# Values three tokens in a row, keys at every third column, and a work order with chance in it

## Chip, cores and metric

The kernel runs on one core of one Trainium2 chip. The metric is the device time of one execution in microseconds (us); the profile shows one such execution, with a span of 1484.0 us and a granted TensorE clock of 0.997 of full speed.

## The reference

Two blocks follow one another. The first is attention over 8 batches, 12 heads, 448 tokens and 64 features, in which queries and keys are first normalised by their root mean square:

```python
q_n, k_n = rmsnorm(q, g_q), rmsnorm(k, g_k)      # x / sqrt(mean(x*x) + 1e-6) * g
scores = q_n @ k_n.T / sqrt(64)
attn = softmax(scores)                            # over the keys
x = (attn @ v), heads side by side                # (3584, 768)
g = x @ w_gate                                    # 768 -> 1536
out = (silu(g) * (x @ w_val)) @ w_out             # 1536 -> 768
```

All inputs are float32 except the three weight matrices, which come as float64 (two 32-bit words each).

The softmax sums over all keys of a head, so the order in which keys are laid out does not matter as long as the values are laid out in the same one. The change rests on this.

## The kernel before

`fast` does the work; `general` is a second version behind a test on the gains, and does not run with these inputs.

**Attention.** Work goes by pairs of heads: 8 x 6 = 48 pairs, `attention(m)`. For a pair, q and k are loaded in pieces of 32 tokens by 32 features (`load`, L728), squared on ScalarE (L754), summed on VectorE (L768) and between partitions on ScalarE (L778, then L782), turned into inverse roots (L678 to L686), scaled on GpSimd (L795), transposed on VectorE in blocks of 32 (L811), and the queries are multiplied by the gains on ScalarE (L814). Now features lie on partitions, 64 for each of the two heads, and tokens along the row: `KT` and `QT`.

The 448 tokens are cut into chunks of 128, 128, 128 and 64 (j = 0 to 3). `scores(j)` (L840) makes the scores of one chunk of keys against all queries, transposed: keys on partitions, queries along the row. Keys are the stationary operand, 64 columns of `KT` at a time, x = 0, 1 for the halves of a chunk and h = 0, 1 for the heads, so four 64x64 matmuls fill the four quadrants of TensorE's array at once. A float32 product takes two passes, so each appears as two weight loads and two matmuls in the trace. ScalarE takes the exponentials (L855), and `weighted(j)` (L916) multiplies them by the values, again in quadrants. The values of a pair are in the tile `v`, tokens on partitions in the same chunks (`load_values`, L744 and L747): token 128 j + p is on partition p. The sums of the exponentials come from a product with a constant (`total`, L947), are inverted (L982), spread over the features (L990 in the first twelve pairs, L1000 after them) and multiplied in (L1005 copies, L1008 joins, L1012 divides).

**Feed-forward.** It goes by blocks of two batches, NB = 4. Its products use a fast matrix multiplication with 15 products for a 3x3 block split; sums of blocks of x are made in `sides` (L1049, L1053), sums of weight blocks once at the start in `convert`, which also turns float64 words into float32 on ScalarE (L1146, L1150) and VectorE (L1168 to L1180), adds on GpSimd (L1202) and stores to DRAM (L1227). There are 24 conversions. The up products are at L1328, the down products at L1502; VectorE and ScalarE read their banks (L1270 to L1276), and results are transposed (L1550) and stored (L1560).

**Stages.** The first 12 pairs run beside the first conversions; then the up products of block 0 beside the other conversions; then the down products of block n beside the 12 pairs for block n + 1, in turn with the up products of block n + 1; last the down products of block 3.

**The order of the work.** Nothing is emitted where it is written. Each piece is given to `Order.add` with its engine, an estimate of its length (`us`), the pieces it comes after, the buffers it takes out of a ring (`takes`) or uses, a due time (`when`) and a `rank`. `Order.run` then plays the program through by these estimates. Pieces of an engine are sorted by `key`, due time less rank. Of an engine's pieces that can start, the first by that key is chosen, unless a later one can start more than 0.4 us earlier; among engines, the earliest start goes first, and within 0.3 us the smaller key. Pieces are emitted in the order in which they are chosen, and that is the order of each engine's queue. Attention pieces of the first twelve pairs mostly have rank 60, reads of the up banks 60, reads of the down banks 20, conversions 20 or, for the first six (`by_bank` false), 0.

## Time and profile before

| what | value |
|---|---|
| time, three runs | 1485.67, 1486.94, 1488.83 us; median 1486.94 |
| span of the profiled execution | 1484.0 us |
| TensorE (PE) busy | 1425.0 us, 96% |
| VectorE (DVE) busy | 916.0 us, 62% |
| ScalarE (ACT) busy | 681.5 us, 46% |
| GpSimd (POOL) busy | 414.1 us, 28% |
| start of the first matmul | 14.7 us |
| start of the first up product | 140.1 us |
| DMA packets | 415921, of these 324164 under 512 bytes |

PE is TensorE's matmul side and PEld its weight loads, which overlap matmuls. SPq is SyncE, which issues most DMAs in a queue of its own. Busy time in a group of instructions is the time in which at least one of them ran; "idle before" is the engine's idle time just ahead of them, with what ended it after the arrow. In a list of waits the columns are the total in us, how many, and the longest one. In a table by stage the numbers after the engines are the granted clock, the mean share of 16 DMA engines, and GB/s.

### The profile page before, as it was taken

Reading aid. Unit: us, or ns where it says so; the run is one execution under the profiler, and the core shown is the slowest. Engines: PE = TensorE matmul, PEld = TensorE weight load, DVE = VectorE, ACT = ScalarE, POOL = GpSimd, SP = SyncE. Lnnn points to the kernel's source line nnn. Section 1 sums busy time; section 2 is a strip of 40 time slices with the busy share of each in tenths; the row PEclk is TensorE's granted clock in tenths of the full one; section 3 lists DMA queues with packets and bytes.
Section 4 is the critical chain, followed back from the end, with each engine's and each line's share of the span. In section 5 each row is a group of like instructions: output and inputs, shape, how many; then the busy total and the mean of one; then the engine's idle time right before and its main releaser. Section 6 shows DMA issues by size and latency. Waiting matters only on the chain.

```text
span 1484.0 us, 19470 instructions
## 1 busy us (share of the span) xinstructions
PE 1425.0 (96%) x6672; PEld 675.4 (46%) x6672; DVE 916.0 (62%) x1405; ACT 681.5 (46%) x1366; POOL 414.1 (28%) x468
## 2 busy tenths in 40 slices
PE   5789999999999999999999999999999999999998
PEld 2334544443444455544444445554444445555553
DVE  4777887877978544355886733454786854432533
ACT  6774544437775322445767422354676532122100
POOL 2454586636444100012544200011343410000000
PEclk9999999999999999999999999999999999999999
DMA  7767999974453432533344432352353442222235
GB/s 165 158 144 236 292 308 341 296 219 90 99 115 85 113 106 71 138 103 90 74 111 110 100 117 73 106 136 77 96 119 85 90 119 89 80 98 73 83 98 107
DMA packets 415921, 193.30 MB, mean 130 GB/s; under 512 B 324164, under 2 KB 397892, under 8 KB 409668
## 3 DMA queue, kind: packets, MB, share of 16 engines
q1 hardware_dynamic: 402688, 190.35, 48.0%
q10 hardware_dynamic: 12996, 1.61, 0.7%
q8 instruction: 55, 0.90, 0.3%
q14 instruction: 54, 0.44, 0.1%
q0 software_dynamic: 128, 0.00, 0.0%
HBM read 157.29 MB, written 34.60 MB: 129 GB/s over the span
## 4 chain that ended last, share of the span: by engine, by line
PE 73%; DVE 3%; ACT 2%; issue 1%; DMA 1%; SPq 1%; ACTq 0%; DVEq 0%
PE mm L1502 22%; PE mm L1328 20%; PE at L1328 20%; PE st L840 6%; PE at L916 5%; PE st L947 1%; ACT spare L1000 1%; ACT es L855 1%; DVE rd L982 1%; DMA out_dram<-spare 0%; SPq L728 0%; DVE ss L782 0%; DMA work<-in_k_dram 0%; DVE ss L768 0%; DVE sums L866 0%
## 5 line engine op out<-in xcount | busy, mean ns | idle before, releaser
L1328 PE MATMUL mm<-xs,ws 128*128 128x448 f32 x960 | 401.2, 540 | 4.4 <-DVE spare L1276 2.2
L1328 PE MATMUL at<-xs,ws 128*128 128x448 f32 x960 | 400.6, 540 | 4.1 <-DVE v L1274 2.6
L1328 PEld LDWEIGHTS mm<-xs,ws 128*128 128x128 f32 x960 | 181.5, 190 | 185.8 <-issue 173.8
L1328 PEld LDWEIGHTS at<-xs,ws 128*128 128x128 f32 x960 | 181.9, 190 | 184.6 <-issue 172.6
L795 POOL TENSOR_TENSOR work<-work,rr 128x448 f32<-128x448 f32 x96 | 105.9, 1122 | 503.5 <-DVE rr L686 245.2
L840 PE MATMUL st<-work 64*64 64x448 f32 (+1 forms) x1536 | 155.1, 508 | 27.3 <-ACT work L814 21.2
L1502 PE MATMUL mm<-gt,ws 128*128 128x448 f32 x448 | 177.2, 545 | 0.0
L1272 DVE TENSOR_TENSOR gt<-gt,mm 128x448 f32<-128x448 f32 x64 | 39.7, 621 | 185.1 <-PE mm L1328 171.3
L1502 PE MATMUL mm<-hs,ws 128*128 128x448 f32 x384 | 152.1, 545 | 0.9 <-DVE ss L684 0.9
L855 ACT ACTIVATE es<-st 128x896 f32<-128x896 f32 x129 | 114.3, 913 | 56.1 <-PE at L916 42.8
L860 POOL TENSOR_TENSOR sums<-es 128x896 f32<-128x896 f32 x36 | 75.7, 2104 | 195.8 <-PE st L947 83.2
L1402 ACT ACTIVATE st<-gt 128x448 f32<-128x448 f32 x96 | 52.4, 547 | 163.8 <-DVE gt L1276 85.9
L1000 ACT COPY spare<-rd 32x224 f32<-32x224 f32 x288 | 108.1, 375 | 35.0 <-DVE rd L982 30.7
L1502 PEld LDWEIGHTS mm<-gt,ws 128*128 128x128 f32 x448 | 82.9, 190 | 84.2 <-issue 81.0
L916 PE MATMUL at<-es,v 64*64 64x448 f32 x1032 | 110.2, 545 | 7.2 <-ACT xs L1005 3.3
L1270 ACT COPY gt<-mm 128x448 f32<-128x448 f32 x80 | 42.5, 531 | 141.5 <-PE mm L1328 141.4
L1502 PEld LDWEIGHTS mm<-hs,ws 128*128 128x128 f32 x384 | 71.1, 190 | 72.9 <-issue 70.9
L840 PEld LDWEIGHTS st<-work 64*64 64x64 f32 x1536 | 50.9, 134 | 108.7 <-issue 38.1
L1270 ACT COPY v<-at 128x448 f32<-128x448 f32 x96 | 51.1, 532 | 83.2 <-PE at L1328 80.0
L860 POOL TENSOR_TENSOR sums<-sums,es 128x896 f32<-128x896 f32 x36 | 78.7, 2187 | 2.8
L811 DVE STREAM_TRANSPOSE work<-work 128x448 f32<-128x448 f32 x96 | 59.2, 627 | 25.2 <-POOL work L795 23.1
L916 PEld LDWEIGHTS at<-es,v 64*64 64x64 f32 x1032 | 39.7, 134 | 67.4 <-issue 57.4
(150 smaller groups left out, 1568.7 us busy)
## 6 DMA issues: line engine op xcount, KB each, us to landing
ws<-up_sides SPq DMA_DIRECT2D x32, 1024.0 KB, 4.9
ws<-down_sides SPq DMA_DIRECT2D x16, 1024.0 KB, 5.0
ws<-down_sides SPq DMA_DIRECT2D x28, 512.0 KB, 4.0
ws<-up_sides SPq DMA_DIRECT2D x16, 768.0 KB, 4.6
work<-in_q_dram SPq DMA_DIRECT2D x192, 56.0 KB, 2.4
work<-in_k_dram SPq DMA_DIRECT2D x188, 56.0 KB, 2.5
out_dram<-spare SPq DMA_DIRECT2D x168, 56.0 KB, 1.9
v<-in_v_dram SPq DMA_DIRECT2D x96, 96.0 KB, 2.5
```

What stands on the lines that cost most here:

```text
L795: nc.gpsimd.tensor_tensor(out=tiles["t", m][:, x], in0=tiles["qk", (m, x)], in1=rr.to_broadcast([P, NC, C]), op=ALU.mult,)
L811: nc.vector.transpose(to, tiles["t", m][:, x].rearrange("p c f -> p (c f)"))
L840: nc.tensor.matmul(st[ds(D * x, D), h, 0:n], tiles["KT", m][rows, ds(P * j + D * of_keys, D)], tiles["QT", m][rows, ds(Q * of_queries, n)] ...
L855: nc.scalar.activation(e, tiles["st", (m, j)][:, :, 0 : S * width(j) // P], AF.Exp)
L860: nc.gpsimd.tensor_tensor(out=to, in0=tiles["e", (m, 0)] if j == 1 else to, in1=e, op=ALU.add)
L916: nc.tensor.matmul(tiles["at", (m, x)][ds(D * h, D), queries], tiles["v", m][rows, j, h], tiles["e", (m, j)][rows, h], start=j == 0, stop= ...
L1000: nc.scalar.copy(inv[ds(D * h + C * to, C), ts(x, Q)], tiles["rd", m][ds(D * h + C * x, C)])
L1270: nc.scalar.copy(to, ps)
L1272: nc.vector.tensor_tensor(out=to, in0=old, in1=ps, op=ALU.add)
L1328: nc.tensor.matmul(ps(), w[:, at, which, c], xs[:, SLOT[x], c], start=fresh and c == 0, stop=c == NC2 - 1, skip_group_check=True,)
L1402: nc.scalar.activation(take(*act, [P, 2, TB])[:, 0, 0:S], to, AF.Silu)
L1502: nc.tensor.matmul(banks[s][:, 0:S], w[:, at, s, g], where[x][:, g], start=fresh and g == 0, stop=g == NG - 1, skip_group_check=True,)
```

## The change

There are three edits.

First, the layout of the values. For the first three chunks, token 3 p + j now goes to partition p of chunk j, so that three tokens that follow one another in memory, 768 bytes, land in one partition's row. The tile is now partition, head, chunk, feature, and one DMA does both heads, where two with rows of 256 bytes were needed. The last 64 tokens stay as they were, loaded twice, once for either half. The estimate of the load goes from 2.4 to 1.8 us.

Second, the keys have to follow: the keys of chunk j, half x, are columns 192 x + j, 192 x + j + 3, and so on, 64 of them, every third column of `KT`. Queries keep their place, so outputs do too.

Third, the order. Every piece that takes no buffer out of a ring gets a shift drawn from -3 to 3 us, added to its key; the draw has a fixed seed, one chosen out of eighty. All conversions have rank 20.

```diff
+        self.chance = random.Random(9)
...
+            shift=self.chance.uniform(-3.0, 3.0) * (not takes),
...
     def key(self, piece):
-        return piece["when"] - piece["rank"], piece["n"]
+        return piece["when"] - piece["rank"] + piece["shift"], piece["n"]
...
         def load_values():
-            x = take("v", m, [P, NJ, 2, D])
-            for h in range(2):
-                rows = v[b, 2 * c + h][0 : P * (NJ - 1)]
-                nc.sync.dma_start(x[:, 0 : NJ - 1, h], rows.rearrange("(j p) d -> p j d", p=P))
+
+            x = take("v", m, [P, 2, NJ, D])
+            rows = v[b][2 * c : 2 * c + 2, 0 : P * (NJ - 1)]
+            nc.sync.dma_start(
+                x[:, :, 0 : NJ - 1].rearrange("p h j d -> p h (j d)"),
+                rows.rearrange("h (p j) d -> p h (j d)", p=P),
+            )
             rows = v[b][2 * c : 2 * c + 2, P * (NJ - 1) :].rearrange("h s d -> s h d")
             for p in (0, D):
-                nc.sync.dma_start(x[ds(p, D), NJ - 1], rows)
-
-        load_v = add("SP", 2.4, ready - 16.0, load_values, takes=[("v", m)], kb=256, early=25.0)
+                nc.sync.dma_start(x[ds(p, D), :, NJ - 1], rows)
+
+        load_v = add("SP", 1.8, ready - 16.0, load_values, takes=[("v", m)], kb=256, early=25.0)
...
                 of_keys, of_queries = (x, 0) if j < NJ - 1 else (0, x)
+                keys = ds(P * j, D)
+                if j < NJ - 1:
+                    keys = slice(
+                        (NJ - 1) * D * x + j, (NJ - 1) * (D * x + D - 1) + j + 1, NJ - 1
+                    )
...
-                        tiles["KT", m][rows, ds(P * j + D * of_keys, D)],
+                        tiles["KT", m][rows, keys],
...
-                        tiles["v", m][rows, j, h],
+                        tiles["v", m][rows, h, j],
...
-        rank = 20.0 if by_bank else 0.0
+        rank = 20.0
```

More of the change, by code (lines that the diff above doesn't have):

```diff
@@ L358, in general @@
             fn()
+import random
 class Order:
```

## The prediction

> **What bounds the kernel now.** I read the engine totals first, then the stages, then who ends the tensor engine's waits, then the loads of the values.

> ```profile
> PE 1425.0 (96%) x6672; PEld 675.4 (46%) x6672; DVE 916.0 (62%) x1405; ACT 681.5 (46%) x1366; POOL 414.1 (28%) x468
> PE 73%; DVE 3%; ACT 2%; issue 1%; DMA 1%; SPq 1%; ACTq 0%; DVEq 0%
> ```

> TensorE is busy for 1425.0 of 1484.0 us, and the chain of waits runs through it. No edit removes or adds a matmul, so the change can only move the 59.0 us in which TensorE is idle, or add idle. Where these lie is told by the busy time by stage (columns: stage, length, then busy us of PE, PEld, DVE, ACT, POOL):

> ```profile
> 15.00:141.00 126.00, 106.21 (x1198) 46.83 (x1190) 95.20 (x158) 86.24 (x163) 62.38 (x94) 0.99 0.72 175
> 141.00:350.00 209.00, 200.50 (x575) 98.78 (x578) 167.25 (x251) 95.43 (x145) 121.82 (x222) 1.00 0.90 274
> 350.00:505.00 155.00, 151.85 (x1016) 64.00 (x1008) 124.86 (x182) 105.50 (x242) 71.29 (x42) 1.00 0.46 102
> ```

> TensorE stands idle 126 - 106.2 = 19.8 us while the first twelve pairs run beside the first weights, 8.5 us in the first block's up products beside the rest of the weights, and 3.2 us in the first mixed stage. Ahead of the first matmul lie 14.7 us and after the last one 7.4 us of stores; both are latency that no edit touches. What is left for all of 505 to 1476 us is 59.0 - 14.7 - 19.8 - 8.5 - 3.2 - 7.4 = 5.4 us. So an order can win at most 19.8 + 8.5 + 3.2 = 31.5 us, nearly all before 350 us. The first matmul's own wait is the 14.7 in the list of waits:

> ```profile
> PE st L840 <- ACT work L814: 21.2, 6, 14.7
> PE at L916 <- ACT xs L1005: 3.3, 2, 2.3
> PE at L916 <- DVE xs L1008: 2.7, 2, 2.1
> PE at L916 <- ACT gt L855: 2.3, 2, 1.3
> PE mm L990 <- DVE rd L982: 2.0, 2, 1.3
> ```

> The other 6.5 us of the first line, and the next four, are waits for the queries' copy, the copy and the join of the sums, an exponential and a reciprocal: short pieces on ScalarE and VectorE that stood behind other work on a strict queue. VectorE is busy for 95.2 and ScalarE for 86.2 of 126 us there, so neither is full; it is their order that lets TensorE wait.

> [...] 190 ns for 128 columns, 134 for 64, 107 for 32 (next fence and its group at L947), so (190 - 134) / 64 = 0.88 ns a column on top of some 78 ns. [...] by its packet records one of 256 bytes takes 18 ns, of 512 bytes 27, of 1024 bytes 46 (medians).

> **The change part by part.**

> *Keys every third column.* Three chunks x two halves x two heads x two passes = 24 of the 32 score loads of a pair, 1152 of these 1536:

> ```profile
> L840 PEld LDWEIGHTS st<-work 64*64 64x64 f32 x1536 | 50.9, 134 | 108.7 <-issue 38.1 <-ACT work L814 26.7 <-ACT es L855 16.6
> L1328 PEld LDWEIGHTS mm<-xs,ws 128*128 128x128 f32 x960 | 181.5, 190 | 185.8 <-issue 173.8
> ```

> The lower end is nothing. For the upper end I double the 56 ns that depend on the columns: 190 ns, just what a 128-column load takes now. Four quadrants load together, once for four matmuls that occupy 376 ns (timeline: sets start every 0.375 us, their loads end after 0.15 us and the load row then idles 0.22 us "issue"). So a load even of 190 ns hides inside a set. It shows only where the slot is short: at the entry from full products, and after the half-wide fourth chunk, whose sets last 0.19 us: two places a pair, 2 x 48 x 56 ns = 5.4 us. I take a quarter, 1.3 us; range 0 to 5.4.

> *Values three tokens in a row.*

> ```profile
> L744 SPq DMA_DIRECT2D v<-in_v_dram x96: 378/484/3534, 7.5 to 1173.4; - x96
> L747 SPq DMA_DIRECT2D v<-in_v_dram x96: 595/607/1903, 8.6 to 1174.6; - x96
> ```

> A pair costs SyncE 2 x 0.484 + 2 x 0.607 = 2.2 us; one issue goes, so 1.7. Its 1024 packets of 256 bytes (1.15 us over 16 engines) become 256 of 768 and 256 of 256; with 36 ns for 768 bytes, between 27 and 46, that is 0.58 + 0.29 = 0.87. So 0.48 us of queue and 0.28 us of transfer go per pair. Where would it show? In the first stage SyncE's queue is the busiest thing but TensorE (in 60:100 its issues leave some 7 us free), and each q and k load queues behind one for values. Twelve pairs x 0.48 = 5.8 us of queue. Yet TensorE waits for no load there, and the squares at L754, the first use of q and k, wait for landings only 8.1 us in all, off TensorE's path by two to three pairs of depth. I take -1 us; bounds 0 and -5.8. In the 36 later pairs q, k and v come long before use: nothing.

> *Half the memory layout.* The weighted sum's loads read rows of 64 adjacent values either way: nothing changes.

> *Converting rank 20 for all.* Only the first six conversions had rank 0. Attention pieces of the first stage have rank 60, so they still go first in a tie; the six move ahead only of things ranked below, of which there are hardly any before 75 us. I take 0, bounds -2 to +2.

> *The order by chance.* Up to 3 us earlier or later in the key of every piece that takes no buffer: squares of the second tensor, roots, scales, the queries' transposes, joins, divides, sides, conversions, and products. A shift decides only between pieces that could start within 0.3 to 0.4 us of each other (that is how run() chooses), so chains stay as they are and full products, tied one to the next, keep their order. Reads of the banks with rank 60 stay ahead. What can change is what stands in front of L814, L1005, L1008 and L982 on ScalarE and VectorE: exactly the owners of the waits above. Such a piece is delayed by one other, by what the rows cost: a conversion's 1.28 us on ScalarE, 1.05 us or 0.75 us on VectorE, an exponential's 0.91. With five to seven waits of 1.0 to 2.3 us (the longest in the list) removed, or as many added, this is worth some 7 to 10 us either way. An arbitrary order would have no sign; one kept out of eighty leans to the good side, if what it was kept by resembles the chip. I take -7: a quarter of 31.5 (7.9), less a little that returns as a wait elsewhere.

> Sum: +1.3 - 1 + 0 - 7 = -6.7, so 1486.9 - 6.7 = **1480 us**.

> **Rivals.** *Order gains nothing net*: the stage is held by VectorE with its 95 us plus latencies, a wait removed returns at the next piece; the parts cancel to about -0 to +1: 1487. For it: several engines are within 30% of each other in the first stage. Against: each single wait has another owner. *Large gain*: half of the 31.5 us goes and SyncE's relief shows, -15.7 - 1: 1470. For it: the engines have room of 30 to 40 us in 15:141. Against: the latency of a pair's chain, square to exponential, repeats whatever the order. *Slower*: an order made for estimates that the chip doesn't keep; first-stage waits grow by a third (+6.6), the loads cost their upper 5.4, the values' gain is hidden: +12, less a little, 1496. It is made likelier by shifts that also act on later stages, which now lose only 5.4 us and so can only get worse.

> **How the numbers follow.** Forecast (3 to 12 us gained) 0.46; large gain 0.16; nothing (within 3 us) 0.14; slower 0.24. So faster 0.62, same 0.14, slower 0.24. The range leaves out about one in ten on either side: 1469 to 1495, the first short of the full large gain, the second close to the upper costs together.

> **What would show it.** Right: TensorE's idle time in 15:350 falls from 28 us to about 21, first product (L1328) starts before 140 us, the waits for L814, L1005 and L1008 shrink; L840's loads stay below 190 ns and the time of score groups unchanged; later stages as before, 190 us from one mixed stage's start to its end. Wrong: L840's loads of 250 ns or more, and gaps ahead of matmuls inside a score group in all three mixed stages, would make the strided keys the main thing; new waits after 505 us would blame the order; a first product later than 141 us with more waits at L1005 or L814 would be the slower rival.

## The result, and the profile after

The change makes the kernel slower: 1501.51 us in the median of four runs (1497.27 to 1503.44), against 1486.69 for the kernel before on the same chip. The ratio is 1.0094, with a 95% interval from 1.0067 to 1.012. The forecast of 1480 and its whole range lie below that.

The profiled execution took 1497.27 us. These are the engine totals, and the table by stage, of the kernel after:

```profile
span 1495.5 us, 19454 instructions
PE 1434.1 (96%) x6672; PEld 690.3 (46%) x6672; DVE 917.7 (61%) x1405; ACT 687.0 (46%) x1370; POOL 409.5 (27%) x468
```

```profile
15.00:141.00 126.00, 108.50 (x1196) 50.81 (x1197) 91.88 (x156) 86.19 (x165) 62.63 (x94) 0.97 0.68 169
141.00:350.00 209.00, 196.02 (x526) 96.39 (x526) 162.12 (x248) 93.72 (x136) 116.33 (x220) 0.97 0.89 273
350.00:505.00 155.00, 149.04 (x994) 65.99 (x993) 120.96 (x167) 105.37 (x240) 73.42 (x44) 0.99 0.43 93
```

The reader is to see two things. TensorE's busy time rose by 1434.1 - 1425.0 = 9.1 us although the number of matmuls, 6672, is the same; its idle time rose only by 11.5 - 9.1 = 2.4 us. And the granted clock, the number after POOL, fell from 0.99, 1.00, 1.00 to 0.97, 0.97, 0.99. The matmuls themselves became slower.

The record of the granted clock in the trace says how. Ahead of the stores at the end, the kernel before has one stretch at half clock, of 3.41 us, at 97.6 us. The kernel after has seven of them, at 31.7, 65.9, 141.0, 270.7, 321.9, 342.3 and 403.8 us. Six more stretches of 3.41 us at half speed can cost up to 6 x 3.41 / 2 = 10.2 us. Each begins within 1.1 us of the end of a wait of TensorE of 1.9 to 3.2 us. The list of TensorE's waits after, from 141 to 350 us, has the longest of these:

```profile
PE st L853 <- ACT work L822: 3.2, 1, 3.2
PE at L1341 <- DVE v L1285: 2.8, 1, 2.8
PE mm L1341 <- DVE gt L1285: 2.8, 1, 2.8
PE at L1341 <- DVE v L1289: 2.6, 1, 2.6
```

(L840 is L853 after the change, L916 L929, L1328 L1341, L1502 L1515, L1272 L1285.) What stood in front is seen in the timeline of the second line, each row with start and length. The product that begins at 260.95 us has ended at 262.62, but VectorE reads its bank only at 269.28; the rows between are conversions, which stood ahead in VectorE's queue (four of them are shown). The next product of that bank has to wait for the read, until 269.95:

```profile
260.95 1.67 PE L1341 MATMUL at<-xs,ws 128*128 128x448 f32 x4
...
266.22 0.76 DVE L1193 CUSTOM_DVE_ANT_0 hs<-hs,st 128x1152 uint16<-128x1152 uint16 x1 [0.17 <-POOL spare L1215]
...
267.01 0.76 DVE L1181 TENSOR_SCALAR st<-hs 128x576 uint32<-128x576 uint32 x1
...
267.81 0.76 DVE L1187 SCALAR_TENSOR_TENSOR st<-hs,st 128x576 uint32<-128x576 uint32 x1
...
268.61 0.75 DVE L1193 CUSTOM_DVE_ANT_0 hs<-hs,st 128x1152 uint16<-128x1152 uint16 x1
269.28 0.61 DVE L1285 TENSOR_TENSOR v<-v,at 128x448 f32<-128x448 f32 x1
...
269.95 1.94 PE L1341 MATMUL at<-xs,ws 128*128 128x448 f32 x3 [2.82 <-DVE v L1285]
```

The busy time by short stages around it shows what follows (the granted clock is the number after POOL). From 271 to 274 us TensorE is always busy, but only six matmuls touch these 3 us, where at 376 ns apart eight would begin:

```profile
267.00:269.00 2.00, 0.13 (x1) 0.00 (x0) 1.92 (x3) 0.00 (x0) 1.84 (x5) 1.00 0.81 311
270.00:271.00 1.00, 1.00 (x3) 0.49 (x4) 0.97 (x2) 0.00 (x0) 0.92 (x2) 0.83 1.03 382
271.00:274.00 3.00, 3.00 (x6) 1.34 (x5) 1.73 (x3) 2.46 (x3) 2.84 (x7) 0.50 1.07 355
```

The texts put on record call such a stretch a half-clock window. Longer ones in the runs below are 6.83, 10.24 and 17.07 us, two, three and five times 3.41. The waits here, 1.9 to 3.2 us, are shorter than the stretch that followed them.

Not every long wait is paid for in this way, and the traces tell which is. In each of the 17 traces of this page the recorded changes of the clock are whole multiples of 3.4133 us apart, to within 3 ns (from the first to the last of the kernel after it is 1460.90 us, 428 times that), so that a trace can be cut into steps of this length. In the kernel after, each of the seven stretches follows a step in which TensorE was idle, by the profile's times of its matmuls, for 2.2 to 3.0 us in all. Three other waits, of 2.6, 2.6 and 2.0 us (ending at 132.5, 289.6 and 366.4 us), lie across the edge of a step, leave at most 1.9 us of idle time in one step, and no half clock follows them. Over all traces together, ahead of the stores at the end, half clock followed a step at full clock with more than 2.02 us of idle time in 61 of 61 cases, one with less than 1.49 us in none of 7027, and one in between in 23 of 63. In the traces of before and after alone it followed each of 8 steps with 2.18 us or more and none of 841 with 1.91 or less.

Where the loss arises is told by the starts of products in the traces (us; the columns are the runs of this page):

| start of | before | after | layout_only | est_only | late_shift_old_start |
|---|---|---|---|---|---|
| first up product | 140.1 | 141.1 | 137.8 | 170.6 | 138.4 |
| first down product | 329.7 | 343.8 | 328.8 | 360.6 | 327.6 |
| up products of block 1 | 505.1 | 520.7 | 504.9 | 530.9 | 504.1 |
| up products of block 2 | 855.3 | 868.8 | 855.6 | 880.8 | 852.2 |
| up products of block 3 | 1205.7 | 1217.2 | 1206.3 | 1230.8 | 1200.6 |
| end | 1484.0 | 1495.5 | 1484.6 | 1509.0 | 1478.9 |

After the change 15.6 us are lost before block 1, 13.1 of them between the first up product and the first down product, and 4.1 us are won in blocks 1 and 2. Single executions differ at the start: the six traces whose compute engines have the order of `layout_only` up to block 1 (that run, `late_shift_old_start` and the four `stall` runs) begin block 1 between 503.2 and 508.9 us. The losses shown here are larger than that.

The weight loads of the scores, and below them the loads of values in `layout_only`, with the shortest, median and longest issue in ns:

```profile
L853 PEld LDWEIGHTS st<-work 64*64 64x64 f32 x1536 | 59.1, 157 | 103.3 <-issue 31.8 <-ACT work L822 30.1 <-ACT es L868 9.6
```

```profile
L749 SPq DMA_DIRECT2D v<-in_v_dram x48: 378/397/4406, 7.5 to 1173.5; - x48
```

The mean of a weight load went from 134 to 157 ns over all 1536 loads. With 133 ns for the 384 of the fourth chunk, the 1152 with every third column take (1536 x 157 - 384 x 133) / 1152 = 165 ns. That is 32 ns more for 64 columns. The kernel before has no load with every third column, so its trace could not show this; why such a load takes longer, no run shows.

### The profile page after: what moved, and what is told of

It reads as the page before. It is cut to its first block, busy times and chain, and to the rows that moved or that the text cites. A ratio compares the mean times of both kernels' runs of the same rounds, so it can differ in the third digit from the quotient of the medians.

```text
span 1495.5 us, 19454 instructions
## 1 busy us (share of the span) xinstructions
PE 1434.1 (96%) x6672; PEld 690.3 (46%) x6672; DVE 917.7 (61%) x1405; ACT 687.0 (46%) x1370; POOL 409.5 (27%) x468
## 4 chain that ended last, share of the span: by engine, by line
PE 74%; DVE 2%; ACT 1%; issue 1%; DMA 1%; DVEq 0%; ACTq 0%
PE mm L1515 23%; PE mm L1341 19%; PE at L1341 19%; PE st L853 7%; PE at L929 6%; PE st L960 1%; DMA out_dram<-spare 0%; ACT es L868 0%; DVE ss L689 0%; ACT spare L1013 0%; DVE rd L995 0%; DVE spare L1563 0%; ACT work L822 0%; DVE rr L691 0%; DVE ss L776 0%
## 5 line engine op out<-in xcount | busy, mean ns | idle before, releaser
L1341 PE MATMUL mm<-xs,ws 128*128 128x448 f32 x960 | 404.8, 544 | 6.4 <-DVE gt L1285 2.8
L1341 PE MATMUL at<-xs,ws 128*128 128x448 f32 x960 | 401.9, 541 | 5.5 <-DVE v L1285 2.8
L1341 PEld LDWEIGHTS mm<-xs,ws 128*128 128x128 f32 x960 | 182.6, 191 | 190.4 <-issue 173.8
L1341 PEld LDWEIGHTS at<-xs,ws 128*128 128x128 f32 x960 | 182.5, 191 | 186.4 <-issue 174.8
L803 POOL TENSOR_TENSOR work<-work,rr 128x448 f32<-128x448 f32 x96 | 99.9, 1059 | 527.2 <-DVE rr L691 300.1
L853 PE MATMUL st<-work 64*64 64x448 f32 (+1 forms) x1536 | 157.1, 515 | 32.0 <-ACT work L822 24.9
L1515 PE MATMUL mm<-gt,ws 128*128 128x448 f32 x448 | 175.2, 543 | 0.0
L1285 DVE TENSOR_TENSOR gt<-gt,mm 128x448 f32<-128x448 f32 x64 | 39.7, 620 | 198.6 <-PE mm L1341 173.4
L1515 PE MATMUL mm<-hs,ws 128*128 128x448 f32 x384 | 153.6, 552 | 0.0
L1515 PEld LDWEIGHTS mm<-gt,ws 128*128 128x128 f32 x448 | 83.7, 190 | 83.7 <-issue 81.3
L929 PE MATMUL at<-es,v 64*64 64x448 f32 x1032 | 112.7, 542 | 4.2 <-DVE xs L1021 4.2
L853 PEld LDWEIGHTS st<-work 64*64 64x64 f32 x1536 | 59.1, 157 | 103.3 <-issue 31.8
L1515 PEld LDWEIGHTS mm<-hs,ws 128*128 128x128 f32 x384 | 72.4, 193 | 73.7 <-issue 72.4
L929 PEld LDWEIGHTS at<-es,v 64*64 64x64 f32 x1032 | 40.9, 134 | 63.5 <-issue 59.5
```

The lines of the kernel that those rows point to most:

```text
L803: nc.gpsimd.tensor_tensor(out=tiles["t", m][:, x], in0=tiles["qk", (m, x)], in1=rr.to_broadcast([P, NC, C]), op=ALU.mult,)
L853: nc.tensor.matmul(st[ds(D * x, D), h, 0:n], tiles["KT", m][rows, keys], tiles["QT", m][rows, ds(Q * of_queries, n)], start=True, stop=True,)
L929: nc.tensor.matmul(tiles["at", (m, x)][ds(D * h, D), queries], tiles["v", m][rows, h, j], tiles["e", (m, j)][rows, h], start=j == 0, stop= ...
L1285: nc.vector.tensor_tensor(out=to, in0=old, in1=ps, op=ALU.add)
L1341: nc.tensor.matmul(ps(), w[:, at, which, c], xs[:, SLOT[x], c], start=fresh and c == 0, stop=c == NC2 - 1, skip_group_check=True,)
L1515: nc.tensor.matmul(banks[s][:, 0:S], w[:, at, s, g], where[x][:, g], start=fresh and g == 0, stop=g == NG - 1, skip_group_check=True,)
```

## Experiments

The first two split the change into its layout and its order. `layout_only` has the new layout of values and keys, and on every compute engine the order of the kernel before, piece for piece; `order_only` has the order of the kernel after with the old layout.

```diff
 layout_only (against the kernel after):
+            shift=0.0,
+        load_v = add("SP", 2.4, ready - 16.0, load_values, ...
+        rank = 20.0 if by_bank else 0.0
```

> The new layout of values and keys, with the order of the kernel before, piece for piece, on every compute engine (no shifts, old ranks, old estimate of the load). Theory A (the new order's waits before 505 us, and the half-clock windows that follow them, are the loss): 1485 to 1490 us, one or two half-clock windows, score weight loads 157 ns in the mean. Rival B (the weight loads with every third column hold the tensor engine up): 1495 us or more, at full clock.

Measured 1485.36 us, ratio to before 0.9984 [0.9974, 0.9995]; two half-clock stretches ahead of the end. The layout costs nothing on balance; it gains some 2 us (0.7 to 3.9 by the interval).

> The new order on every compute engine, with the old layout of values and keys. Theory A: 1496 to 1504 us, six or more half-clock windows, waits of 2.5 to 3.2 us for VectorE while the first block's up products run. Rival B: 1483 to 1490 us.

Measured 1504.80 us, just above theory A's range; ratio 1.0132 [1.0101, 1.0164], seven stretches ahead of the end. The whole loss is the order's. Strided keys, rival B, are out.

The order has three causes: shifts, rank, and the plan's estimate of the load. In `no_chance` only the shifts are taken out of the kernel after; in `chance_late` they act only late:

```diff
 chance_late:
-            shift=self.chance.uniform(-3.0, 3.0) * (not takes),
+            shift=self.chance.uniform(-3.0, 3.0) * (not takes) * (when >= 490.0),
```

> The changed kernel with all shifts at zero: new layout, load estimated at 1.8 us, rank 20 for all conversions. Theory A: 1482 to 1491 us, close to before, since the shifts and not the ranks or the estimate made the waits. Rival C (rank or estimate moved the order as much as the shifts): 1495 us or more, or a first stage unlike that of before.

Measured 1499.60 us, ratio 1.0079 [1.0061, 1.0098]. My theory A fell in this part: without a single shift the kernel is as slow as with them. Rank or estimate do it too. The waits are others: 7.2 us of them, the longest 4.2, are for loads of weight sums (`ws<-up_sides`), of which the kernel after has none.

> The changed kernel with shifts only for pieces due at 490 us or later by the plan. Theory A: the first 505 us as in the kernel without shifts, then some 2 us won per later block as in the changed kernel (first up product of block 1 to that of block 2 in 348 us, not 350): 1480 to 1487 us, at most two half-clock windows. Rival (the later gain comes from the layout, not from the shifts): same as the kernel without shifts within 2 us.

Measured 1494.30 us, ratio 1.0049 [1.0032, 1.0066]. The number was missed, since the start was slow without shifts too, but against `no_chance` late shifts gain 5.3 us, and block 1 to block 2 takes 348.1 us in place of 349.9.

The next four separate rank from estimate. `est_only` and `rank_only` change one line each of `layout_only`; `est24_chance` takes only the estimate back in the kernel after; `late_shift_old_start` adds the late shifts to `layout_only`.

```diff
 est_only:   load_v = add("SP", 1.8, ...)      in place of 2.4
 rank_only:  rank = 20.0                       in place of 20.0 if by_bank else 0.0
```

> New layout, no shifts, old ranks; only the plan's estimate of the load of values is 1.8 instead of 2.4 us. Theory D (the estimate alone re-orders the first 505 us on every engine and makes the long waits): 1495 to 1502 us, first up product of block 1 at 517 us or later, half-clock windows after waits of 2.5 us or more. Rival E (the rank did it): 1483 to 1488 us.

Measured 1509.49 us, ratio 1.0148 [1.0131, 1.0165], worse than the whole change. One number in the plan, which changes the order of the instructions and none of them, moved the first up product from 137.8 to 170.6 us. TensorE's waits in it:

```profile
PE st L853 <- ACT work L822: 17.7, 3, 14.8
PE at L929 <- DVE xs L1021: 15.6, 4, 7.3
PE st L1003 <- DVE rd L995: 7.0, 1, 7.0
```

The second and third line are a join of 7.3 us' wait and an inversion of 7.0. In the timeline ahead of the join VectorE runs reductions, transposes and sums of blocks of x (L1062, L1066), which stand ahead of it in this order. Half clock holds for 51.2 us in all ahead of the end (3.41 three times, 6.83 twice, 10.24 and 17.07), against 6.8 us in `layout_only`.

> New layout, no shifts, old estimate; only the rank of the first six conversions is 20 instead of 0. The tensor engine's queue is the same as with the new layout alone, and VectorE's differs in short stretches. Theory D: 1483 to 1489 us. Rival E: 1495 us or more.

Measured 1485.59 us, ratio 0.9991 [0.9984, 0.9997]. The rank is harmless, as forecast; TensorE's queue is the same.

> The changed kernel with the old estimate of 2.4 us for the load: new layout, shifts, rank 20. Theory D in its strict form (the wrong estimate, and not another order as such, makes the waits): 1480 to 1488 us. Rival F (any re-ordering of the first 505 us costs on the mean, since the order of before was already a picked one): 1493 us or more.

Measured 1494.87 us, ratio 1.0042 [1.003, 1.0054]. So the strict form of theory D fell as well: with the old estimate, the shifts alone spoil the start. Block 1 begins at 518.2 us, 14.9 us later than in `rank_only`, which is this kernel without shifts; the times agree, since the whole kernel is 9.3 us slower although its later blocks are 4.9 us faster. (Its fifteen runs spread from 1489.08 to 1498.57 us; the trace is of a run of 1494.87.) Two independent causes give the same kind of loss, and they do not add up: with the estimate of 1.8, block 1 begins at 520.3 us without shifts and at 520.7 with them.

> New layout, old estimate and ranks, shifts only for pieces due at 490 us or later by the plan. The first 490 us as with the new layout alone, the later blocks as with shifts: some 5 us under the new layout alone, by the gain that late shifts had over none (1499.6 to 1494.3): 1479 to 1482 us, faster than both kernels. Rival (that gain hangs on the state of the plan at 490 us): 1483 to 1488 us.

Measured 1480.03 us, ratio 0.9944 [0.9928, 0.9961]: faster than both kernels. From block 1 to block 3 the up products' starts are 696.5 us apart, 4.9 us less than in `layout_only` (701.4). Waits of TensorE from 505 us on, first of `layout_only`, then of this run:

```profile
PE mm L1515 <- ACT spare L1283: 2.8, 2, 1.4
PE mm L1341 <- DVE spare L1289: 2.2, 3, 0.7
PE st L853 <- ACT es L868: 1.2, 4, 0.4
```

```profile
PE mm L1341 <- DVE spare L1289: 1.4, 2, 0.7
PE st L853 <- ACT work L822: 0.2, 1, 0.2
PE st L853 <- ACT es L868: 0.2, 1, 0.2
```

The first line, one bank copy late in each of two blocks, is gone, and of the third most: 3.6 us with the second run's L822 counted. (Of the line at L1341 one wait of 0.7 us ends at 504.1 us in this run, outside the window, so its change means nothing.) Between block 1 and block 3 TensorE also changes 66 times, not 72, between full products and small ones; that the other 1.3 us come from this is not shown.

Is the start of before a special order, or is 1.8 a special number? `est20` puts 2.0 in its place; `seed2` is the kernel after with another draw.

> New layout, no shifts, old ranks, estimate of the load 2.0 us. Theory F (the start of before was a picked order, and nearly any other is worse): 1490 us or more, with waits at other places than with 1.8. Rival (1.8 is special because it is too short): 1483 to 1488 us.

Measured 1514.93 us, ratio 1.0187 [1.0154, 1.022]: 1.8 is not special.

> The changed kernel with another draw of the shifts. Theory F: also slower than before, 1490 to 1510 us, with another pattern of waits in the first 505 us, and the later blocks within 3 us of the changed kernel's. Rival (this one draw was bad): 1486 us or less.

Measured 1510.95 us, just above the range; ratio 1.0175 [1.0141, 1.0209], with waits of up to 8.0 us for L1021. Its later blocks do not repeat the gain of the draw that was kept: from block 1 to block 3 they take 699.6 us, against 696.5 in the kernel after and 699.9 in `no_chance`. Theory F holds in each of the six runs that re-order the start on all engines (estimates of 1.8 and 2.0, 1.8 with rank 20, that with either draw, and the first draw with 2.4): they begin block 1 13 to 31 us later than `layout_only`. Of the two draws, the one that was kept is the better. With the old estimate it is slower than no draw (1494.87 against 1485.59 us); with the new one the runs show no clear difference (1501.51 and 1499.60).

The last group measures the half clock by itself. On top of `layout_only`, useless adds of 0.42 us stand on VectorE ahead of one bank read, in the up products of blocks 1 to 3, groups 0 to 2, where the clock is otherwise full. They add work and change nothing that is computed.

```diff
+                if n > 0 and g < 3 and which == 0 and x in (5,):
+                    for _ in range(16):
+                        nc.vector.tensor_tensor(out=scratch, in0=scratch, in1=scratch, op=ALU.add)
                 read(how, to, old, ps())
```

> New layout alone, with 17 useless adds on VectorE ahead of one bank read at 9 places in the up products of blocks 1 to 3, where no other wait is; each should stop the tensor engine for about 3 us. Theory G (a wait near 3 us is followed by a window of 3.4 us at half clock, which costs up to 1.7 us more): about nine new half-clock windows, and a time over the new layout alone that exceeds the idle time put in by 9 to 15 us (some 28 of idle, 37 to 43 in all). Rival H (a wait costs its own length only): excess within 3 us.

Measured 1485.66 us, ratio 0.9996 [0.9984, 1.0007]: 17 adds ahead of the read of product 13, 7.2 us, made no wait at all, so it says nothing of theory G. It shows that 153 adds, 65 us of VectorE's time, are free where slack is.

> The same with 13 adds at 18 places, so that each wait is about 1.5 us and the sum about the same. Theory G: hardly any new half-clock window, and a time over the new layout alone equal to the idle time put in (some 27 us) within 4 us. Rival H: the same as that, so only the pair of runs tells them apart.

Measured 1504.71 us, ratio 1.012 [1.0089, 1.0151]. Of the 18 places only the 9 at product 5 made waits, of 1.8 us; no half-clock stretch followed any.

> New layout alone, with 16 useless adds ahead of the bank read of product 5 at 9 places (13 adds there gave 9 waits of 1.8 us and no half-clock window): waits of about 3.1 us each, 28 us in all. Theory G: several new half-clock windows after them, and a cost over the new layout alone of 28 us plus 1.3 to 1.7 us for each window, 36 to 44 us in all: 1521 to 1530. Rival H: 28 to 31 us, 1513 to 1517, at full clock.

Measured 1525.41 us, ratio 1.0252 [1.0234, 1.0271].

> The same with 21 adds: waits of about 5.2 us, 47 us in all. Theory G: nine new half-clock windows, 58 to 64 us in all: 1543 to 1550. Rival H: 47 to 50 us, 1532 to 1536.

Measured 1558.60 us, ratio 1.0475 [1.045, 1.0501]; more than either theory said, since one wait brought more than one stretch.

The three lines, of `stall_short`, `stall16` and `stall21`, in the lists of waits (each has one wait more, of 0.6 us, than the nine):

```profile
PE mm L1342 <- DVE gt L1290: 17.0, 10, 1.8
```

```profile
PE mm L1342 <- DVE gt L1290: 29.4, 10, 3.2
```

```profile
PE mm L1342 <- DVE gt L1290: 50.1, 10, 5.5
```

From the first up product of block 1 to the last of block 3 `layout_only` takes 881.5 us:

| run | takes | over layout_only | the nine waits | the rest | half-clock stretches after them |
|---|---|---|---|---|---|
| stall_short | 900.3 | 18.8 | 16.4 | 2.4 | none |
| stall16 | 921.1 | 39.6 | 28.8 | 10.8 | 5 of 3.41 us |
| stall21 | 955.4 | 73.9 | 49.5 | 24.4 | 8 of 6.83 and 1 of 3.41 us |

So a wait of 1.8 us cost its length and 0.27 us. Of the waits of 3.2 us five in nine, of those of 5.5 us nine in nine were followed by half clock. Taking off 2.4 us for the nine restarts, the rest in `stall_short`, 8.4 us are left for 5 x 3.41 = 17.1 us at half clock, and half of 17.1 is 8.5. In `stall21` 22.0 us are left for 58.1 us at half clock; of these 13.4 passed while TensorE still waited, and half of the other 44.7 is 22.3. Theory G holds, and rival H is out.

Which five of the nine equal waits were followed by half clock is again told by the steps of 3.413 us: those five leave 2.0 to 2.4 us of idle time in one step, the other four at most 1.97. A wait of 1.8 us can't leave more than that in one step, wherever it falls.

> New layout, old estimate, rank 20 for all conversions, shifts only for pieces due at 490 us or later. If the parts add up (rank 20 alone within 2 us of the new layout alone, late shifts some 5 us): 1478 to 1482 us. Rival (the parts don't add, since the plan's state at 490 us differs): 1483 us or more.

Measured 1480.77 us, ratio 0.9951 [0.9933, 0.9969]: the rank adds nothing measurable.

## Why the prediction was wrong

The forecast of direction and size was wrong. By its own steps:

- **Strided keys, +1.3 us (0 to 5.4).** Right. The loads grew by 32 ns, not the 56 of the upper end, which was my estimate. From 505 us on, at full clock, the longest in the kernel after took 175 ns, and they hide inside sets: at 734.48 us four take 0.18 us, and the load row then idles 0.19 us. At an entry from full products the second set of scores of `layout_only` starts 458 ns after the first, where it was 427 (medians). From block 1 to block 3, which holds 24 of the 48 pairs, `layout_only` takes 701.4 us and the kernel before, with the same order, 700.6; `order_only` and the kernel after differ by 0.4. For 48 pairs that makes 0.8 to 1.6 us, an estimate.
- **Values, -1 us (0 to -5.8).** Right on SyncE: 0.397 + 2 x 0.607 = 1.6 us a pair, against 1.7 forecast, and a packet of 768 bytes took 36 ns, as taken. `layout_only` is some 2.4 us faster than before by its ratio (1 - 0.9984), with the strided keys paid, so this gain is nearer 3 to 4 us than 1. Where it arises is not shown: the first up product starts 2.3 us earlier than before in this trace, but among the six traces with this start it lies anywhere from 137.8 to 143.5 us.
- **Rank 20, 0 us.** Right: `rank_only` is within 0.1% of `layout_only`.
- **The estimate of the load.** This is the first step that failed, by not being there. I worked out the new load's cost on SyncE and never asked what the plan does with 1.8 in place of 2.4. Alone it costs 24 us against `layout_only`. The estimate is even the better one, since the load takes 1.6 us; it helped nothing.
- **The order by chance, -7 us.** The second step that failed, twice over. First, "one kept out of eighty leans to the good side": it was kept among orders that begin with a disturbed start, and each such start that I ran is slower than the old one. With the old estimate the shifts of the start cost 14.9 us (`est24_chance` against `rank_only`); late shifts gain about 5. I had it the other way round: "later stages, which now lose only 5.4 us and so can only get worse". Those stages gained 4.1 us, while the start, where I placed nearly all the gain, lost 15.6. The steps behind it failed as well. "Reads of the banks with rank 60 stay ahead" did not hold on the chip: the read at 269.28 us stood behind conversions. And a piece was not "delayed by one other": between the end of that product and its read VectorE ran eight pieces of conversions, in 6.7 us.
- **"Worth some 7 to 10 us either way", by the idle time.** TensorE's idle time rose by 2.4 us only, which is within that size, with the sign wrong: it rose by 4.5 and 2.8 us in the two stages from 141 to 505 us and fell elsewhere. The term that was missing is the clock. I took matmul time as fixed ("the change can only move the 59.0 us in which TensorE is idle, or add idle"), and busy time rose by 9.1 us. The granted clock of 0.94 in the kernel before, from 80 to 100 us, after a wait of 2.1 us, would have told me that a long wait can be paid for again after it; three earlier waits of 2.1 to 2.6 us in that trace were not.
- **The slower rival** (1496 us, 24%) had the side right, and "estimates that the chip doesn't keep" is part of it. It was too small by 5.5 us, and named the strided keys' upper cost where the half clock was the matter.

What makes the old start good is not settled: no run shows which of its placements counts, only that six other orders of it, by two kinds of disturbance, are all slower. The four runs of the kernel after also differ among themselves as the clock does: 1497.27 and 1499.86 us at a mean clock of 0.991, 1503.44 at 0.987 and 1503.15 at 0.986.

## What to carry to other kernels

When a planner writes the order, an estimate is part of the program: change one and compare the queues before pricing anything else, for its own cost may be the smallest part. Shake an order stage by stage: the same shifts that cost 15 us at the old start won 5 us later, and another draw won next to nothing there. On TensorE look at the longest waits and not at their sum only: here a wait that left more than 2 us of idle time in one of the clock's steps of 3.41 us was paid for again by up to 1.7 us a step at half clock (in `stall16` 8.4 us for five), and one of 1.8 us, in a busy stretch, was not.
